# Windowed attention and a gated layer on one core: q and k of a head set in one transfer each, heads h and h+2 paired, far rows of v in one transfer, a few steps in another order

## The chip, the cores and the metric

The kernel runs on one core of a Trainium2 chip. The metric is device time in microseconds (us). Three runs of the kernel before took 621.86, 622.98 and 624.29 us; their median is 622.98 us. A profile is one more execution, recorded instruction by instruction. PE is the matmul engine (PEld its weight load), DVE the vector engine, ACT the scalar engine, POOL the general one, SP the engine that issues most transfers; SPq and ACTq are the issuing queues of SP and ACT.

## The reference, cut to what matters

```python
# q, k, v: 4 batches, 8 heads, 768 positions, 64 values a head; n_global = 8, n_local = 96
scores = q @ k.T / sqrt(64) - slope[h] * dist           # dist: i - j, or n_local for a global key outside the window
keep   = (j < n_global) | ((i - j >= 0) & (i - j < n_local))
a      = softmax(where(keep, scores, -1e9))
x      = (a @ v), heads side by side: 3072 x 512
h      = x @ w_in                                       # 3072 x 2048
g      = h * tanh(log1p(exp(h)))
out    = g @ w_out                                      # 3072 x 512
```

Since a position sees only the last 96 keys and the first few, scores are computed against a window of keys and 32 "far" keys from the start of the sequence.

## The kernel before, in words

The 3072 positions are cut into 12 chunks `ci` of 256 (three per batch), each of two blocks of 128. The heads of a chunk are cut into two sets `g` of four heads, so there are 24 loads of q and k, numbered `G = 2 ci + g`. `load_qk(G)` (step `q`, L161 to L176) brings a set into two tiles: `qr`, 128 partitions by 2 heads by 256 positions, and `kr`, 128 partitions by 2 heads by 416 keys. Partitions 0 to 63 hold the 64 values of one head of a pair (`j = 0`), partitions 64 to 127 those of the other (`j = 1`); `a2` numbers the two pairs. A pair is heads `2 a2` and `2 a2 + 1` of the set. q comes from `qT` by one transfer (L172) whose source pattern has the outer count 128; k comes from `kd`, which holds each head's 416 keys in order and holds them twice, by two transfers, one for each `j` (L175), each with the outer count 64. For the first chunk of a batch only keys from 128 on are loaded. The very first `j = 1` half goes through ACT's queue, all else through SP's. Each of `qr` and `kr` has three buffers.

For the first three chunks (`CF32`, loads 0 to 5) the score matmuls (`scores`, step `s`, L407) read `qr` and `kr` as they are, in f32. For later chunks `high_q`, `low_q`, `high_k`, `low_k` (steps `a` to `d`) first split them into f16 halves on ACT, DVE and POOL (`ws<-qr`, `wc<-kr`). Then `largest` (step `t`, L421, DVE) adds the mask and finds the row maximum, `exps` (`y`, L430, ACT) exponentiates, the weights are turned, by PE for the first chunks (`P`, L460, copied out by `F`) and by a DMA transpose later (`X`, L450, into `AT`), and `weigh` (`W`, L482 and L486, PE) multiplies by v. `window_v` (step `x`) gathers the v rows of the window; for the second and third chunk it reads the 32 far rows twice by two transfers (L234). The masks are made once, one 128 by 128 tile (`L`, tile `mb0`) and one 128 by 256 tile (`M`, tile `mb`) a head: on ACT, or, where a step carries a prime, on DVE for heads 0 to 3 and on POOL for heads 4 to 7 (`masked`, L284 to L288). The gated layer follows chunk by chunk: `i` (L549, `ph`), its activation on ACT and DVE, and `o` (L605, `po`). The weights come in 32 pieces of 512 KB (step `w`, L322 and L324) and are converted by ACT, DVE and POOL; step `B` (L353) is DVE's first touch of a piece.

Nothing is scheduled by a planner: a string `PROGRAM` lists all steps, and each engine and each queue does its part of them strictly in that order. SP's queue therefore holds the q, k, v and weight loads, the transposes `X` and `V` and the stores, in one line.

Of the kernel before, what the change touches and what calls it, by code (L numbers as in the profile page):

```python
# [16 lines left out]
ALU = mybir.AluOpType  # L17
# [3 lines left out]
P = 128  # L21
NLMAX = 97
NGMAX = 32
NPREV = 96
# [18 lines left out]
def tile_kernel(ctx, tc, qd, kd, qT, kT, v, n, w_in, w_out, out):  # L43
# [33 lines left out]
    with ExitStack() as st:  # L77
        windowed(st, tc, locals())
# [36 lines left out]
def windowed(st, tc, loc):  # L115


    nc = tc.nc
    L = NS()
    L.__dict__.update(loc)  # L120
    B, H, D, S, NB, NCC, NFB = L.B, L.H, L.D, L.S, L.NB, L.NCC, L.NFB
    CH, KW, DM, DFF = L.CH, L.KW, L.DM, L.DFF
    W = 2 * P
    GH = H // 2
    NCHB = S // CH
    NC = B * NCHB
    NFP = NFB // 2
    OWN = NPREV + NGMAX
# [16 lines left out]
    def copy(out, in_, scale, other=False):  # L145

        if other:
            nc.vector.tensor_scalar(out, in_, scale, None, op0=ALU.mult)  # L148
        else:
            nc.scalar.activation(out, in_, AF.Copy, scale=scale)  # L150
# [12 lines left out]
    def load_qk(G):  # L163
        if G >= 2 * NC:
            return
        ci, g = divmod(G, 2)
        b, c = divmod(ci, NCHB)
        o = OWN if c == 0 else 0
        pairs = slice(g * GH // 2, (g + 1) * GH // 2)
        qr = raws.tile([P, GH // 2, CH], F32, name="qr", bufs=3)  # L170
        kr = raws.tile([P, GH // 2, KW], F32, name="kr", bufs=3)
        nc.sync.dma_start(qr, L.qT[b].rearrange("(a j) d s -> (j d) a s", j=2)[:, pairs, c * CH:(c + 1) * CH])  # L172
        for j in range(2):
            half = slice(j * D, (j + 1) * D)
            (nc.scalar if G == 0 and j else nc.sync).dma_start(kr[half, :, o:], L.kd[ci, half].rearrange("p (a j) w -> p a j w", j=2)[:, pairs, j, o:])  # L175
        raw[G] = (qr, kr)  # L176

    def first_key(G):
        return OWN if (G // 2) % NCHB == 0 else 0
# [31 lines left out]
    def halves_v(tile_):  # L211
        return tile_.rearrange("p t m -> p (t m)").bitcast(F16).rearrange("p (t x m) -> p t x m", t=2, x=2)
# [10 lines left out]
    def window_v(ci):  # L223
        b, c = divmod(ci, NCHB)
        vc = stk.tile([P, 2, DM], F32, name="vc")
        if ci < CF32:
            far = L.v[b, 0:NGMAX, :]
            if c == 0:
                nc.sync.dma_start(vc[0:NPREV, 1], L.v[b, P - NPREV:P, :])
                nc.sync.dma_start(vc[NPREV:P, 1], far)  # L230
            else:
                nc.sync.dma_start(vc[0:NPREV], L.v[b, c * CH - NPREV:(c + 1) * CH - NPREV, :].rearrange("(t p) m -> p t m", p=P)[0:NPREV])
                for t in range(2):
                    nc.sync.dma_start(vc[NPREV:P, t], far)  # L234
            vcmp[ci] = vc
            return
        vo = vown[ci]
        vc = halves_v(vc)
        for t in range(2):
            if c == 0 and t == 0:  # L240
                continue
            src = vo[NGMAX:P, 0] if t else vown[ci - 1][NGMAX:P, 1]
            nc.sync.dma_start(vc[0:NPREV, t], src)
            nc.sync.dma_start(vc[NPREV:P, t], vo[0:NGMAX, 0] if c == 0 else vcmp[ci - 1][NPREV:P, 1])
        vcmp[ci] = vc


    UNIT = L.ISC
# [33 lines left out]
    mb0 = cp.tile([P, H, P], BF16, name="mb0")  # L282

    def masked(out, in_, h, other):  # L284
        if other and h >= H // 2:
            nc.gpsimd.tensor_scalar(out, in_, -L.slopes[h] * UNIT, None, op0=ALU.mult)
        else:
            copy(out, in_, -L.slopes[h] * UNIT, other)  # L288

    def mask_own(h, other=False):  # L290
        masked(mb0[:, h, :], d0, h, other)

    def mask_far(h, other=False):
        masked(mb[:, h, :], rel, h, other)
# [90 lines left out]
    def shape(t):  # L385
        ci, g, blk, a2 = where(t)
        first = ci % NCHB == 0 and blk == 0
        return ci, g, blk, a2, first, 1 if first else 2
# [21 lines left out]
    def largest(t):  # L410
        ci, g, blk, a2, first, nk = shape(t)
        w = nk * P
        sc = pend[t]
        if (ci, blk) not in stat:
            stat[ci, blk] = [at.tile([P, H], F32, name=f"{n}{blk}") for n in ("rs", "nm")]
        nm = stat[ci, blk][1]
        A = at.tile([P, 2, W], F32, name="A", bufs=3)
        for j in range(2):
            h = g * GH + 2 * a2 + j
            m = mb0[:, h, :] if first else mb[:, h, :]  # L420
            nc.vector.tensor_tensor_reduce(out=A[:, j, 0:w], in0=sc[j][:, 0:w], in1=m, scale=-1.0 / (UNIT if ci < CF32 else UNIT * SQ), scalar=3.0e38, op0=ALU.add, op1=ALU.min, accum_out=nm[:, h:h + 1])  # L421
        pend[t] = A

    def exps(t):
        ci, g, blk, a2, first, nk = shape(t)
        rs, nm = stat[ci, blk]
        A = pend[t][:, :, 0:nk * P]
        for j in range(2):
            h = g * GH + 2 * a2 + j
            nc.scalar.activation(A[:, j], A[:, j], AF.Exp, bias=nm[:, h:h + 1], scale=-1.0, accum_out=rs[:, h:h + 1])  # L430

    def halved(t):
# [36 lines left out]
    def weigh(t):  # L469
        ci, g, blk, a2, first, nk = shape(t)  # L470
        AT = pend.pop(t)
        if (ci, blk) not in pavs:
            pavs[ci, blk] = ps.tile([P, DM], F32, name=f"pav{blk}", bufs=1)
        pav = pavs[ci, blk]
        vs = [vown[ci][:, blk]] if nk == 1 else [vcmp[ci][:, blk], vown[ci][:, blk]]
        for j in range(2):
            h = g * GH + 2 * a2 + j
            cols = slice(h * D, (h + 1) * D)
            n, last = 0, 3 * nk - 1
            if ci < CF32:  # L480
                for kk in range(nk):
                    nc.tensor.matmul(pav[:, cols], AT[:, j * nk + kk, :], vs[kk][:, cols], start=(kk == 0), stop=(kk == nk - 1))  # L482
                continue
            for kk in range(nk):
                for x, y in ((0, 0), (0, 1), (1, 0)):
                    nc.tensor.matmul(pav[:, cols], AT[:, (x * 2 + j) * nk + kk, :], vs[kk][:, y, cols], start=(n == 0), stop=(n == last))  # L486
                    n += 1
# [149 lines left out]
    v1 = cp.tile([1, NALL], F32, name="v1")  # L637
# [4 lines left out]
    def checks(i):  # L642
# [22 lines left out]
    E = mybir.EngineType  # L665
    acts = {
        "q": load_qk, "v": load_v, "w": load_w,
        "a": lambda p, other=False: high_q(p - 1, other), "b": lambda p: low_q(p - 1), "c": lambda p, other=False: high_k(p - 1, other),
        "d": lambda p, other=False: low_k(p - 1, other), "N": units, "h": high_v, "l": low_v, "x": window_v,
        "K": lambda i: masks_far() if i else masks_own(), "L": mask_own, "M": mask_far,  # L670
        "s": scores, "t": largest, "y": exps, "g": high_a, "p": low_a, "X": turn_a, "W": weigh,
        "I": identity, "P": turn_p, "F": turned, "O": turn_x32,
        "R": rows, "T": high_x, "U": low_x, "V": turn_x,
# [2 lines left out]
        "z": high_g, "Z": low_g, "o": moe_out, "Q": evacuate, "Y": store, "f": lambda i: flags(), "k": checks,  # L676
    }
    PROGRAM = """
        I0 K0 L2 K1 L4 L0 L3 v0 w2 q1 x0 s0 t1 y1 M3 P1 L1' t0 s2 B2 F1' f0 M0 M2 M1 L5 y0 A2 t3 t2 P0 W1 y3 P3 q2 w0 v1 w1 q3 x1 s4 F0' M6' M4' M7' L7' M5'
        L6 F3' y2 P2 W3 t5 t4 S2' F2' y4 y5 s6 P4 P5 W0 W2 F4 t6 t7 y6 P6 s8 F6' C2 t9 t8 B0 S0 F5 y7 W6 W5 P7 W4 R0 B1 y9 A0 F7 y8 s10 P9 O0 W7 P8 t11 S1'  # L680
        t10 A1 C0 R1 F9 y11 F8 y10 P11 s12 P10 O1 w3 w4 q4 w7 w6 q5 w5 v2 w12 x2 w8 v3 w13 w10 w14 w9 w15 t12 t13 T0 F11 D2 D0 y12 y13 E2 E0 T1' U0 F10' U1
        W8 s14 W9 P12 i0 P13 t14 A3' B3 y14 S3 S4 F12' t15 B4 C3 y15 j0 u0 n0 F13 W10 P14 s16 W11 W13 P15 W12 G0 D3' C1 t17 D1 y17 A7 F15 S7 r0 B7 t16 F14'
# [6 lines left out]
        j12 A25' B19 E17 H11 S22' G12 A19 z11 C24 Z11' o3 i4 i17 D24 B22 E24 C22 E20 S19 u12 j4 D22 u4 n4 c7 n12 G4 S25' C19 B25 a7' C25 d7' b7 o11 s24 i18  # L689
        D19 r12 J17 r4 E22' H4 N0 t24 D25' A26' H12 t25 z4' J18 y25 A21 z12 E25' l3 E19' Z12' S26' B21 B26 Z4' i13 s26 i5 o12 j13 y24 G13 u13 S21 j5 A28 o4  # L690
        i20 q9 w30 w27 S28' C21 C26 D26' E26' B23 B28 t26 A30 u5 n5 D21 C28 g25 r5 n13 B30 G5 J20' S30' g24 E21' y26 r13 A23 H5 S23' i19 i6 p25' z5 A27 C23
        J19' D23 E23' c8' C30 H13 j6 u6 D28 g26 z13 B27 p26' Z5 Z13' D30' G6 E28' E30 p24 d8 w29 X25 w31 v4 X24 q8 x3 X26 i14 o5 i21 j14 u14 n6 r6 n14 S27
        r14 G14 H6 t27 S31 a8 i7 C27 y27 J21 z6 j7 u7 D27 B29 b8 S29' E27 Z6' H14 z14 Z14 i15 s28 o13 o14 o6 n7 r7 j15 u15 a9 n15 A31' A29' B31 G7 H7 t28
        C29 C31 G15 D31' z7' Z7' r15 D29 j16 u16 j17 y28 u17 n17 n16 r16 g27 H15 g28' p28' G16 z15' t29 E29 E31 H16 Z15 z16' G17 p27' Z16' o7 s30 o15 j18
        u18 y29 Q0 r17 q10 X28 Y0 o16 t30 g29' b9 H17 z17' Z17' h4' a11' t31 p29 y30 n18 r18 j19 u19 c9 G18 H18 d9' G19 z18' Z18 n19 Q1 r19 H19 j21 j20 o17
# [38 lines left out]
        n94 r94 o92 H94 j95 u95 G95 n95 z94 r95 o93 Z94 H95 z95 o94 k1 Z95' o95 k2 Q11  # L734
    """
    load_qk(0)
    nc.scalar.preload_act_table_set("natural_log_exp_and_others")
    with tc.manual_schedule(engines={E.DVE, E.Activation, E.Pool, E.PE, E.SP}):
# [156 lines left out]
```

## Time and profile before

| | us |
|---|---|
| median of three runs | 622.98 |
| the profiled execution's own time | 621.52 |
| its span in the trace | 619.7 |
| PE busy in it | 603.1 |
| DVE, ACT, POOL busy | 463.2, 444.8, 163.3 |
| PE's first matmul | 6.06 after the span's start |

The profiled execution's time is 1.8 us more than its span and 1.5 us under the median. In a row of the timeline the columns are start, duration, engine, line, operation, tiles written <- tiles read, shapes, count, and in brackets the idle time before it with what ended it. A row on waits reads: engine, line, what it waited for, total us, times, longest. A row on transfers reads: tiles, queue, count, KB each, median us from issue to landing. A row on a stretch of time has each engine's busy time, PE's clock, the share of the sixteen DMA engines that was busy and the GB/s they moved.

### The profile page before, as it was taken

The page shows a single profiled execution, that of the slowest core. Times are in us where ns is not written, and L with a number is a line of the kernel's source. Part 1 is how long each engine was busy: PE and PEld are TensorE (multiplying, and loading weights), DVE is VectorE, ACT ScalarE, POOL GpSimd, SP SyncE. Part 2 cuts the span into 40 slices and gives each one's busy share as a digit, 9 for nine tenths or more (in the row PEclk, how much of TensorE's full clock was granted, in tenths as well). Part 3 has the DMA queues.
Part 4 walks back from the last instruction along what each step waited for, and adds up shares of the span by engine and source line. Part 5 has one row for each costly group of instructions (what it writes and reads, how often), then busy time and mean ns, then how long its engine had stood idle before and what let it go on. Part 6 is the DMA issues. An engine that isn't in the chain of part 4 may idle for free.

```text
span 619.7 us, 13567 instructions
## 1 busy us (share of the span) xinstructions
PE 603.1 (97%) x5066; PEld 417.0 (67%) x5066; DVE 463.2 (75%) x1198; ACT 444.8 (72%) x1106; POOL 163.3 (26%) x135
## 2 busy tenths in 40 slices
PE   4999999999999999999999999999999999999996
PEld 3888857686556767576776775776667766766672
DVE  5899999989998789687776777775885866462443
ACT  5999888779886767576876757766866865665652
POOL 3031434033222350224133204223124332301020
PEclk9999999999999999999999999999999999999998
DMA  8998465235365859226357554474374344320001
GB/s 222 285 264 280 142 201 150 71 110 133 69 142 132 161 103 217 53 63 144 69 90 196 100 129 103 102 176 62 68 160 83 65 71 105 87 35 1 34 2 38
DMA packets 123014, 73.02 MB, mean 118 GB/s; under 512 B 91712, under 2 KB 112192, under 8 KB 122944
## 3 DMA queue, kind: packets, MB, share of 16 engines
q1 hardware_dynamic: 122800, 71.97, 49.8%
q8 instruction: 41, 0.67, 0.5%
q10 hardware_dynamic: 144, 0.15, 0.1%
q14 instruction: 29, 0.24, 0.1%
HBM read 39.85 MB, written 6.29 MB: 74 GB/s over the span
## 4 chain that ended last, share of the span: by engine, by line
PE 77%; DVE 11%; ACT 4%; issue 4%; DMA 2%; SPq 0%; POOL 0%; DVEq 0%; ACTq 0%; POOLq 0%
PE ph L549 33%; PE po L605 30%; PE sc L407 5%; PE pav L486 3%; PE pav L482 2%; DVE gf L587 2%; DVE gf L583 2%; DMA wts<-w_in 1%; DMA AT<-hl 1%; DVE ws L357 1%; PE po L460 1%; DVE A L421 1%; ACT A L430 1%; PE pav L605 1%; DVE ws L353 1%
## 5 line engine op out<-in xcount | busy, mean ns | idle before, releaser
L549 PE MATMUL ph<-xT,wts 128*128 128x256 f16 x2304 | 263.6, 273 | 0.2 <-POOL wts L154 0.2
L549 PEld LDWEIGHTS <-wts 128*128 128x128 f16 x2304 | 222.8, 98 | 35.5 <-issue 1.9
L605 PE MATMUL po<-wts,gt 128*128 128x512 f16 x1056 | 238.7, 379 | 0.8 <-DVE gt L148 0.5
L605 PEld LDWEIGHTS <-gt 128*128 128x128 f16 x1152 | 110.1, 98 | 126.8 <-issue 2.9
L154 POOL TENSOR_TENSOR gt<-gf,gt 128x512 f16<-128x512 f32 x55 | 67.5, 1229 | 278.7 <-DVE gt L148 142.7
L567 ACT ACTIVATE e<-ph 128x512 f32<-128x512 f32 x90 | 53.1, 590 | 89.9 <-PE ph L549 89.7
L430 ACT ACTIVATE A<-A,nm 128x256 f32<-128x256 f32 (+1 forms) x192 | 91.6, 478 | 29.1 <-DVE nm L421 29.1
L587 DVE CUSTOM_DVE_ANT_0 gf<-gf,u 128x512 f32<-128x512 f32 x96 | 79.5, 829 | 42.9 <-ACT u L579 41.7
L583 DVE SCALAR_TENSOR_TENSOR gf<-e,ph 128x512 f32<-128x512 f32 x90 | 61.1, 682 | 52.4 <-ACT e L567 51.3
L421 DVE CUSTOM_DVE_ANT_0 A<-sc,mb 128x256 f32<-128x256 f32 (+1 forms) x192 | 68.3, 396 | 16.9 <-PE sc L407 13.8
L154 POOL TENSOR_TENSOR hl<-A,hl 128x512 f16<-128x512 f32 (+1 forms) x36 | 44.8, 1250 | 74.2 <-DVE hl L148 31.8
L571 ACT ACTIVATE u<-e 128x512 f32<-128x512 f32 x96 | 59.9, 625 | 1.7
L579 ACT ACTIVATE u<-u 128x512 f32<-128x512 f32 x96 | 59.4, 624 | 1.8
L575 ACT ACTIVATE u<-u 128x512 f32<-128x512 f32 x96 | 59.5, 623 | 1.7
L154 POOL TENSOR_TENSOR wts<-ws,wts 128x512 f16<-128x512 f32 x20 | 25.7, 1292 | 72.1 <-ACT wts L150 37.6
L150 ACT ACTIVATE gt<-gf 128x512 f16<-128x512 f32 x44 | 27.4, 623 | 22.0 <-DVE gmax L587 22.0
L430 ACT ACTIVATION_READ_ACCUMULATOR A<-A,nm 128x1 f32 x192 | 36.0, 188 | 0.0
L486 PEld LDWEIGHTS <-AT 128*128 128x128 f16 x792 | 28.7, 98 | 7.2 <-issue 1.9
L154 DVE TENSOR_TENSOR hl<-A,hl 128x512 f16<-128x512 f32 (+1 forms) x36 | 30.0, 834 | 2.0 <-ACT hl L150 1.7
L154 DVE TENSOR_TENSOR gt<-gf,gt 128x512 f16<-128x512 f32 x41 | 28.9, 706 | 3.3 <-ACT gt L150 2.9
L407 PE MATMUL sc<-wc,ws 64*128 64x256 f16 (+1 forms) x432 | 28.2, 262 | 0.7 <-DVE nm L421 0.7
L486 PE MATMUL pav<-vo,AT 128*128 128x64 f16 x432 | 27.5, 193 | 0.0
(124 smaller groups left out, 600.3 us busy)
## 6 DMA issues: line engine op xcount, KB each, us to landing
kr<-kd SPq DMA_DIRECT2D x32, 208.0 KB, 4.2
qr<-qT SPq DMA_DIRECT2D x24, 256.0 KB, 4.2
wts<-w_in SPq DMA_DIRECT2D x12, 512.0 KB, 8.3
wts<-w_out SPq DMA_DIRECT2D x12, 512.0 KB, 8.9
out<-ob SPq DMA_DIRECT2D x11, 512.0 KB, 3.8
vr<-v SPq DMA_DIRECT2D x9, 512.0 KB, 5.1
vc<-vo SPq DMA_DIRECT2D x15, 192.0 KB, 3.3
kr<-kd SPq DMA_DIRECT2D x15, 144.0 KB, 5.1
```

The lines of the kernel that those rows point to most:

```text
L154: (nc.vector if other else nc.gpsimd).tensor_tensor(out, in_, high, op=ALU.subtract)
L407: nc.tensor.matmul(sc[j][:, a2, 0:w], x[half, a2, rows_], y[half, a2, col0:col0 + w], start=(n == 0), stop=(n == len(terms) - 1))
L421: nc.vector.tensor_tensor_reduce(out=A[:, j, 0:w], in0=sc[j][:, 0:w], in1=m, scale=-1.0 / (UNIT if ci < CF32 else UNIT * SQ), scalar=3.0e3 ...
L430: nc.scalar.activation(A[:, j], A[:, j], AF.Exp, bias=nm[:, h:h + 1], scale=-1.0, accum_out=rs[:, h:h + 1])
L486: nc.tensor.matmul(pav[:, cols], AT[:, (x * 2 + j) * nk + kk, :], vs[kk][:, y, cols], start=(n == 0), stop=(n == last))
L549: nc.tensor.matmul(ph[:, j, :].rearrange("p (b t) -> p b t", b=2), wv4[:, 2 * fb, x, c * P:(c + 1) * P], xT[:, :, y * NCC + c, :], start=( ...
L571: nc.scalar.activation(u, mish[m]["e"], AF.Square, bias=0.5)
L575: nc.scalar.activation(mish[m]["r"], mish[m]["u"], AF.Ln, bias=0.25 / RS, scale=1.0 / RS)
L579: nc.scalar.activation(r, r, AF.Exp, scale=-1.0)
L583: nc.vector.scalar_tensor_tensor(gf, mish[m]["e"], 0.5, mish[m]["h"], op0=ALU.add, op1=ALU.mult)
L587: nc.vector.tensor_tensor_reduce(out=gf, in0=gf, in1=mish[m]["r"], scale=SG / (SV * SW * RS), scalar=0.0, op0=ALU.mult, op1=ALU.max, accum ...
L605: nc.tensor.matmul(pos[ci][t], gt[:, x, j, t * P:(t + 1) * P], wv4[:, 2 * fb + 1, y, :], start=(fb == 0 and n == 0), stop=(fb == NFB - 1 a ...
```

## The change

1. `load_qk` issues one transfer for q and one for k. Both read packed arrays (`qd`, `kd`) through a hand-written source pattern with the counts 2, 64 and one run of 512 or 832 values: the outer count is the two halves of the partitions, the next one the 64 values of a head, and the run the two neighbouring heads of a half, 2048 bytes of q and 3328 of k. The destination is 128 partitions by the run. The first chunk's unused 128 keys are now loaded too (3328 instead of twice 1152 bytes a partition). The very first k goes through ACT's queue whole.
2. So that a half's heads are neighbours, a pair is now heads h and h+2 of the set (`head`): `j` picks the upper or lower two, `a2` the one of them. All steps that index heads follow.
3. The far rows of v for two blocks come by one transfer that reads them twice.
4. A primed mask is made on DVE for every head; POOL makes none.
5. In `PROGRAM`, `M3 L1'` stand ahead of `t1` instead of behind it, and `C30` ahead of `c8'` instead of behind it.

```diff
-        b, c = divmod(ci, NCHB)
-        o = OWN if c == 0 else 0
-        pairs = slice(g * GH // 2, (g + 1) * GH // 2)
         qr = raws.tile([P, GH // 2, CH], F32, name="qr", bufs=3)
         kr = raws.tile([P, GH // 2, KW], F32, name="kr", bufs=3)
-        nc.sync.dma_start(qr, L.qT[b].rearrange("(a j) d s -> (j d) a s", j=2)[:, pairs, c * CH:(c + 1) * CH])
-        for j in range(2):
-            half = slice(j * D, (j + 1) * D)
-            (nc.scalar if G == 0 and j else nc.sync).dma_start(kr[half, :, o:], L.kd[ci, half].rearrange("p (a j) w -> p a j w", j=2)[:, pairs, j, o:])
+        for dst, src, w, queue in ((qr, L.qd, CH, nc.sync), (kr, L.kd, KW, nc.sync if G else nc.scalar)):
+            both = bass.AP(src.tensor, ci * P * H * w + g * GH * w, [[D * H * w + GH // 2 * w, 2], [H * w, D], [1, GH // 2 * w]])
+            queue.dma_start(dst.rearrange("p a w -> p (a w)"), both)
         raw[G] = (qr, kr)
+
+    def head(g, a2, j):
+        return g * GH + j * (GH // 2) + a2
...
-                for t in range(2):
-                    nc.sync.dma_start(vc[NPREV:P, t], far)
+                nc.sync.dma_start(vc[NPREV:P], far.unsqueeze(1).broadcast_to([NGMAX, 2, DM]))
...
     def masked(out, in_, h, other):
-        if other and h >= H // 2:
-            nc.gpsimd.tensor_scalar(out, in_, -L.slopes[h] * UNIT, None, op0=ALU.mult)
-        else:
-            copy(out, in_, -L.slopes[h] * UNIT, other)
+        copy(out, in_, -L.slopes[h] * UNIT, other)
...
-            h = g * GH + 2 * a2 + j
+            h = head(g, a2, j)
...
     PROGRAM = """
-        I0 K0 L2 K1 L4 L0 L3 v0 w2 q1 x0 s0 t1 y1 M3 P1 L1' t0 s2 B2 F1' f0 ...
+        I0 K0 L2 K1 L4 L0 L3 v0 w2 q1 x0 s0 M3 L1' t1 y1 P1 t0 s2 B2 F1' f0 ...
...
```

SP's queue at the start of the program, before (loads 0 to 2; `vo` and `vc` are v, `wts` a weight piece; the half of load 0 that ACT issues is not in it):

```order
L62 DMA n_i<-n 128x4
L172 DMA qr<-qT 128x2x256
L175 DMA kr<-kd 64x2x288
L209 DMA vo<-v 128x2x512
L322 DMA wts<-w_in 128x4x256
L172 DMA qr<-qT 128x2x256
L175 DMA kr<-kd 64x2x288 x2
L229 DMA vc<-v 96x512
L230 DMA vc<-v 32x512
L172 DMA qr<-qT 128x2x256
L175 DMA kr<-kd 64x2x416 x2
```

The same place now:

```order
L62 DMA n_i<-n 128x4
L171 DMA qr<-qd 128x1x512
L208 DMA vo<-v 128x2x512
L317 DMA wts<-w_in 128x4x256
L171 DMA qr<-qd 128x1x512
L171 DMA kr<-kd 128x1x832
L228 DMA vc<-v 96x512
L229 DMA vc<-v 32x512
L171 DMA qr<-qd 128x1x512
L171 DMA kr<-kd 128x1x832
```

One transfer a load is gone from the line; load 0's k has left it altogether, and the shapes shown are those of the destination.

DVE before, from the copies of the turned weights of tiles 0 and 3 (`AT<-po`) to the row maxima of tile 5 (`po_196` and `po_204` are buffers of `po`, `mb_98` is the tile `mb0`, `nm` the maxima):

```order
L148 TENSOR_SCALAR AT<-po_196 128x256
L148 TENSOR_SCALAR AT<-po_204 128x512
L421 ISA A,nm_152<-sc,mb_98 128x128
L421 ISA nm_152 128x1
L421 ISA A,nm_152<-sc,mb_98 128x128
```

The same place now:

```order
L148 TENSOR_SCALAR AT<-po_194 128x256
L148 TENSOR_SCALAR mb<-e 128x256 x3
L148 TENSOR_SCALAR mb_98<-u 128x128
L148 TENSOR_SCALAR mb<-e 128x256
L148 TENSOR_SCALAR AT<-po_202 128x512
L416 ISA A,nm_152<-sc,mb_98 128x128
```

Five masks that POOL made stand now on DVE, between two copies for which PE's next `weigh` waits.

More of the change, by code (lines that the diff above doesn't have):

```diff
@@ L428, in exps @@
         for j in range(2):
-            h = g * GH + 2 * a2 + j
+            h = head(g, a2, j)
             nc.scalar.activation(A[:, j], A[:, j], AF.Exp, bias=nm[:, h:h + 1], scale=-1.0, accum_out=rs[:, h:h + 1])
@@ L476, in weigh @@
         for j in range(2):
-            h = g * GH + 2 * a2 + j
+            h = head(g, a2, j)
             cols = slice(h * D, (h + 1) * D)
@@ L678, in windowed @@
     PROGRAM = """
-        I0 K0 L2 K1 L4 L0 L3 v0 w2 q1 x0 s0 t1 y1 M3 P1 L1' t0 s2 B2 F1' f0 M0 M2 M1 L5 y0 A2 t3 t2 P0 W1 y3 P3 q2 w0 v1 w1 q3 x1 s4 F0' M6' M4' M7' L7' M5'
+        I0 K0 L2 K1 L4 L0 L3 v0 w2 q1 x0 s0 M3 L1' t1 y1 P1 t0 s2 B2 F1' f0 M0 M2 M1 L5 y0 A2 t3 t2 P0 W1 y3 P3 q2 w0 v1 w1 q3 x1 s4 F0' M6' M4' M7' L7' M5'
         L6 F3' y2 P2 W3 t5 t4 S2' F2' y4 y5 s6 P4 P5 W0 W2 F4 t6 t7 y6 P6 s8 F6' C2 t9 t8 B0 S0 F5 y7 W6 W5 P7 W4 R0 B1 y9 A0 F7 y8 s10 P9 O0 W7 P8 t11 S1'
@@ L691, in windowed @@
         i20 q9 w30 w27 S28' C21 C26 D26' E26' B23 B28 t26 A30 u5 n5 D21 C28 g25 r5 n13 B30 G5 J20' S30' g24 E21' y26 r13 A23 H5 S23' i19 i6 p25' z5 A27 C23
-        J19' D23 E23' c8' C30 H13 j6 u6 D28 g26 z13 B27 p26' Z5 Z13' D30' G6 E28' E30 p24 d8 w29 X25 w31 v4 X24 q8 x3 X26 i14 o5 i21 j14 u14 n6 r6 n14 S27
+        J19' D23 E23' C30 c8' H13 j6 u6 D28 g26 z13 B27 p26' Z5 Z13' D30' G6 E28' E30 p24 d8 w29 X25 w31 v4 X24 q8 x3 X26 i14 o5 i21 j14 u14 n6 r6 n14 S27
         r14 G14 H6 t27 S31 a8 i7 C27 y27 J21 z6 j7 u7 D27 B29 b8 S29' E27 Z6' H14 z14 Z14 i15 s28 o13 o14 o6 n7 r7 j15 u15 a9 n15 A31' A29' B31 G7 H7 t28
```

## The prediction

> **What bounds the kernel now.** I read the page's first two parts first, then the waits, then the transfers.
>
> ```profile
> PE 603.1 (97%) x5066; PEld 417.0 (67%) x5066; DVE 463.2 (75%) x1198; ACT 444.8 (72%) x1106; POOL 163.3 (26%) x135
> PE   4999999999999999999999999999999999999996
> ```
>
> PE is busy in all but the first and the last slice: what feeds PE is hidden except at the start. The waits say the same, PE's own row first:
>
> ```profile
> PE sc L407 <- DMA kr<-kd: 6.1, 1, 6.1
> PEld L486 <- DMA AT<-hl: 1.3, 3, 0.6
> DVE ws L353 <- DMA wts<-w_in: 2.1, 1, 2.1
> ```
>
> PE waits for a load of k once, at the start; all later loads of q and k come in time, and the transposes `AT` cost its weight load 1.3 us in all. So loads cost nothing as long as they stay quick. How quick they are, and how many engines carry them:
>
> ```profile
> q1 hardware_dynamic: 122800, 71.97, 49.8%
> q10 hardware_dynamic: 144, 0.15, 0.1%
> ...
> kr<-kd SPq DMA_DIRECT2D x32, 208.0 KB, 4.2
> qr<-qT SPq DMA_DIRECT2D x24, 256.0 KB, 4.2
> wts<-w_in SPq DMA_DIRECT2D x12, 512.0 KB, 8.3
> ...
> AT<-hl SPq DMA_TRANSPOSE x72, 3.3
> ...
> kr<-kd ACTq DMA_DIRECT2D x1, 144.0 KB, 3.6
> ```
>
> Queue q10 carried one transfer only, ACT's half of the first k: 64 partitions of 2 pieces are 128 packets, and 16 more stand there, one for each DMA engine that had a share to report. A transfer of 144 to 256 KB that is dealt out so lands in about 4 us.
>
> ```profile
> 9.50:15.50 6.00, 4.95 (x32) 3.23 (x30) 4.30 (x19) 4.21 (x17) 2.29 (x3) 1.00 1.10 233
> 16.50:18.50 2.00, 2.00 (x18) 1.62 (x19) 1.24 (x4) 1.73 (x8) 0.00 (x0) 1.00 1.06 393
> 62.00:558.00 496.00, 493.29 (x4275) 336.77 (x4275) 389.48 (x953) 363.24 (x892) 141.81 (x109) 1.00 0.50 112
> ```
>
> The last two columns are the busy share of the sixteen DMA engines and GB/s. Fully busy they move 393 GB/s at best, 24.6 per engine, and 233 in a worse stretch, 14.6 per engine. From 62 to 558 us they are half busy.
>
> **The change: one load of q and k.** It is now 128 partitions x (2048 + 3328) bytes = 688,128 bytes in two transfers. All that counts is over how many engines they are dealt out. Over sixteen it is 43,008 bytes each, 1.75 us (2.9 at the worse rate). Over two it is 344,064 bytes each, 14.0 us (23.6). No row of the trace shows a transfer of the new kind, so these are the ends. In every transfer of before the source and the destination begin with the same count (128, 96, 64 or 32), which sixteen divides. In the new ones the source begins with 2, the two halves, and the destination with 128. If a transfer is cut along that first count, the only equal cut that fits both is into two: partitions 0 to 63 by one engine, 64 to 127 by another. A cut into sixteen would need the queue to look through to the second count of one side only. I take two engines, at 24.6 GB/s (two engines alone crowd each other less than sixteen did in the worse stretch): 14.0 us a load.
>
> The Trainium skill, page "DMA: Bandwidth & Descriptors", section "Why a DMA increments its semaphore by 16 and not by 1", says it as a rule: a transfer from SP or ACT runs on the largest number of engines, at most 16, that divides the outermost count (other than 1) of both patterns. By the row of q10 alone the load would be 1.75 us on sixteen engines, by the rule 14.0 us on two. The trace agrees as far as it goes (64 and 64, sixteen reports); no run so far has an outer count under 16.
>
> **The start.** The first six loads feed PE directly. The first and the sixth use:
>
> ```profile
> 6.06 1.22 PE L407 MATMUL sc<-kr,qr 64*128 64x128 f32 x8 [6.06 <-DMA kr<-kd]
> ...
> 45.48 1.14 PE L407 MATMUL sc<-kr,qr 64*128 64x256 f32 x8
> ...
> 1.20 0.42 SPq L172 DMA_DIRECT2D qr<-qT  x1
> ```
>
> What a transfer takes beside its data: the q load issued at 285.8, in a quiet stretch, lands 3.0 us after its issue, and 256 KB at 393 GB/s are 0.7 us of that, so 2.3.
>
> ```profile
> DMA to landing us min/median/max: 3.0/3.0/3.0
> ```
>
> The first scores then start at 1.2 + 2.3 + 14.0 = 17.5, not 6.06. The loads stand in one line with v and weights. Up to the sixth load there are nine other transfers of 512 KB (1.33 us of each engine) and 0.77 MB of v windows (2.0 us): 14 us. It lands at 1.2 + 2.3 + 6 x 14.0 + 14 = 101.5 and is used at 45.5 now. PE's order is fixed and nothing later can go first, so the start costs 56 us; the other engines have no slack of that size, since each is in the same order behind the same scores.
>
> **The later eighteen loads.** Sum over the stretch 62 to 558: each engine is busy for 0.50 x 496 = 248 us; the two engines lose 18 x 1.75 and gain 18 x 14.0, and come to 468 of 496 us. So a load mostly fits, but never lands in under 2.3 + 14.0 = 16.3 us. Seven of the eighteen are used sooner after their issue, the first and the last of them:
>
> ```profile
> 139.59 0.57 SPq L172 DMA_DIRECT2D qr<-qT  x1
> ...
> 147.20 0.62 ACT L150 ACTIVATE ws<-qr 128x512 f16<-128x512 f32 x1
> ...
> 405.15 0.47 SPq L172 DMA_DIRECT2D qr<-qT  x1
> 412.34 0.61 ACT L150 ACTIVATE ws<-qr 128x512 f16<-128x512 f32 x1
> ```
>
> The seven gaps, from the issue to the first instruction on the tile, are 7.6, 10.6, 8.6, 12.9, 9.0, 6.8 and 7.2 us, 62.7 together, so 7 x 16.3 - 62.7 = 51 us are late even if each is alone in the line. They are not alone:
>
> ```profile
> 194.82 0.57 SPq L172 DMA_DIRECT2D qr<-qT  x1
> ...
> 201.43 0.58 SPq L172 DMA_DIRECT2D qr<-qT  x1
> ...
> 206.25 0.58 SPq L172 DMA_DIRECT2D qr<-qT  x1
> ...
> 208.26 4.43 SPq L450 DMA_TRANSPOSE AT<-hl  x2
> ...
> 216.93 0.25 PE L486 MATMUL pav<-vc,AT 128*128 128x64 f16 x3
> ...
> 402.36 0.72 SPq L172 DMA_DIRECT2D qr<-qT  x1
> ```
>
> Three loads issued within 12 us are 42 us of the two engines, to 194.8 + 2.3 + 42 = 239; the transposes issued at 208.3 stand behind them and are used by 216.9, 22 us too late, of which 5.7 is in the sum already. The load at 405.15 stands behind that at 402.36, 11 us more, and there is such a pair near 236 and a transpose behind a load near 432: some 49 us more together. Against that, ACT and DVE have a few us in hand when they stop, and each stop lets the line drain: 7 x 4 us less. Between 51 - 28 = 23 and 51 + 49 = 100 I take 85, near the upper end, since the two engines are 94% full there.
>
> **The small edits.** Masks: POOL's rows and the nearest DVE rows are
>
> ```profile
> 7.72 2.67 POOL L286 TENSOR_SCALAR mb<-e 128x256 bf16<-128x256 f32 x3 [6.24 <-DVE e L279]
> ...
> 7.88 0.32 DVE L148 TENSOR_SCALAR mb<-u 128x128 bf16<-128x128 f32 x1
> ...
> 13.66 0.42 DVE L148 TENSOR_SCALAR AT<-po 128x256 f32<-128x256 f32 x1
> 14.37 0.69 DVE L148 TENSOR_SCALAR AT<-po 128x512 f32<-128x512 f32 x1 [0.29 <-PE po L460]
> ```
>
> Four masks at 0.32 to 0.42 and one at 0.32 are 1.6 to 2.0 us on DVE, ahead of the copy at 14.37, where DVE had 0.29 free. The long wait for load 1 (to about 35 us instead of 14) covers them: 0. Without that cover they cost 1.3 to 1.7. `M3` and `L1'` ahead of `t1`: 0.3 on ACT and on DVE before the first maxima, covered by the 11 us wait for the scores, else 0.3. The swap of `C30` and `c8'` moves two neighbours on DVE: at most their 0.7 us either way, taken as 0. The far rows save two issues of about 0.3 us on SP, and the loads one issue each; nobody waits for SP's issuing today, so 0. The 128 KB more of each first chunk are in the 14.0.
>
> **Sum.** 621.5 (the profiled execution: span 619.7 and 1.8 around it) + 56 + 85 = 762.5, and 1.5 more for the median: 764 us.
>
> **The rivals.**
> - *Two engines, but only the start pays.* Loads are often issued far ahead, the DMA engines are half idle, and stops at one place give slack to the next. Then 623 + 56 = 679. Against it are the seven short gaps, which no idle time helps. 0.13.
> - *Two engines at the worse rate.* At 14.6 GB/s a load takes 23.6 us: the sixth lands at 159, 114 late, and the later stretch asks for 248 - 31 + 425 = 642 of 496 us, 146 late: 623 + 260 = 883. For it: rows of 9.5 to 15.5 us are of just such loads. Against it: fourteen engines are then out of the way. Anything over 825 has 0.10.
> - *The other side: sixteen engines after all.* If the queue cuts along the 128 partitions (or sees through the 2), a load takes 1.75 us and lands as now. Then SP issues the first weight piece 0.8 us sooner, behind 128 KB more (0.3 us), and DVE's wait for it, 2.1 us above, ends 0.5 sooner; the masks cost 1.3 to 1.7 behind it, partly under PE's own backlog. 623 - 0.5 + 0 to 1.7: about 623, no change. It decides at the very first k: q10 would show 128 + 16 packets instead of 128 + 2. For it: every row so far shows sixteen. Against it: every row so far also has equal first counts, and no cut into sixteen fits a first count of 2. 0.09.
>
> **How the numbers follow.** The forecast, 685 to 825, has 0.68. Its low end is a start of 45 (some transfers let through beside the loads) and 23 later with the median's 623, 691; its high end 60 and 140. With the rival at 679 the range 675 to 825 holds 0.81. About 0.5% (3.1 us) is what a measurement of this kernel can tell. Faster by more: 0.02, only within the last rival, if fewer and larger pieces free more than the masks cost. Same: 0.06, the rest of that rival but 0.01. Slower: 0.92.
>
> **What would show it.** Right: q10 with 130 packets; PE's first scores near 17.5 and the sixth load's near 101; loads that land 16 us or more after their issue; waits of PE on `sc` for DMA of some 50 us, then of ACT and DVE for `qr` and `kr` and of PE for `AT`. Wrong: 144 packets on q10 and loads that land in about 4 us (then the third rival), scores as late as said but no waits for loads after 110 us (the first), or a first load that takes 24 us (the second).

## The result and the profile after

The changed kernel takes 813.98 us, the median of six runs (810.60 to 816.46); the kernel before takes 622.42 us (six runs, 620.76 to 625.49). The ratio is 1.306, 95% interval 1.302 to 1.311. The forecast was 764, range 675 to 825. The profiled execution has a span of 814.7 us.

The page after, PE's busy time, its slices, the granted clock and the queue that carried the very first k:

```profile
PE 646.8 (79%) x5066; PEld 441.2 (54%) x5066; DVE 461.1 (57%) x1203; ACT 446.5 (55%) x1106; POOL 158.0 (19%) x130
PE   0575679996987980892996949899575899999997
PEclk9998579998997995795998989989878899999999
q10 hardware_dynamic: 130, 0.43, 0.2%
```

PE's row of nines has holes from the start to about 650 us (32 of the 40 slices). q10, which carries one transfer only, shows 128 pieces and 2 reports where it would show 16 for sixteen engines. The clock falls in the slices behind the holes; PE's busy time is 647 us instead of 603 for the same 5066 matmuls.

PE's waits after:

```profile
PE pav L481 <- DMA AT<-hl: 58.0, 7, 17.2
PE sc L402 <- DMA kr<-kd: 35.5, 5, 9.1
PE sc L402 <- DMA qr<-qd: 19.2, 1, 19.2
PE po L600 <- DVE gt L148: 11.8, 2, 11.0
PE pav L481 <- DMA vc<-vc: 11.7, 1, 11.7
```

The single wait of 6.1 us became 55 us for q and k at the start (`sc`), and 58 us for `AT`, the transposed weights, later. `AT` is no load of q or k: it is a transfer of another kind that comes late. The later loads of q and k are late too, for ACT and DVE, as all engines' waits after show:

```profile
DVE wc L148 <- DMA kr<-kd: 20.0, 1, 20.0
...
ACT ws L150 <- DMA qr<-qd: 15.6, 3, 13.7
```

The first scores and those that read the sixth load, in PE's timeline after:

```profile
19.21 1.23 PE L402 MATMUL sc<-kr,qr 64*128 64x128 f32 x8 [19.21 <-DMA qr<-qd]
...
109.73 2.08 PE L402 MATMUL sc<-kr,qr 64*128 64x256 f32 x8 [5.37 <-DMA kr<-kd]
```

They stood at 6.06 and 45.48 before: 13.2 and 64.3 us later. The stretches of the windows view show why. Its last three columns are PE's clock, the busy share of the sixteen transfer engines, and GB/s:

```profile
12.00:18.00 6.00, 0.00 (x0) 0.00 (x0) 0.00 (x0) 0.00 (x0) 0.00 (x0) 1.00 0.13 51
...
86.00:90.00 4.00, 0.00 (x0) 0.00 (x0) 0.00 (x0) 0.00 (x0) 0.00 (x0) 0.50 0.13 52
```

A share of 0.13 is 2 of 16 engines, and 51 GB/s are 25.5 each. PE, DVE, ACT and POOL do nothing in these stretches; two transfer engines alone are at work. In the second stretch the granted clock is 0.50, after the idle time ahead of it. The trace has no entry for the clock before 61 us, so the 1.00 of the first row is no reading: the eight matmuls on 64x256 at 22.11 take 2.08 us, as those at 109.73 do at half the clock, and 1.14 before.

SP's issuing at the start, in the timeline after (start, duration):

```profile
1.22 0.72 SPq L171 DMA_DIRECT2D qr<-qd  x1
1.98 0.42 SPq L208 DMA_DIRECT2D vo<-v  x1
2.45 5.38 SPq L317 DMA_DIRECT2D wts<-w_in  x1
7.87 6.55 SPq L171 DMA_DIRECT2D qr<-qd  x1
14.46 3.81 SPq L171 DMA_DIRECT2D kr<-kd  x1
```

Here an issue takes 0.4 to 0.7 us as long as the two engines have little in hand, then up to 6.6 us: SP is held up in the issuing itself. Its issues take 471.6 us together (231 of them), before 211.1 us (257).

To see where the 195 us arise, the start of some of PE's steps (`s`, `W`, `o` as in `PROGRAM`) in the trace after less that in the trace before: `s20`, on the sixth load, 64; `W24`, the first `weigh` on transposed weights, 85; `W39` 112; `W45` 132; `W57` 155; `W74` 194; the last step, 195. So 64 us come from the first six loads and some 130 us from the eighteen later ones, the last of which is issued at 614.

### The profile page after: what moved, and what is told of

The parts are those of the page before. It is cut to its first block, busy times and chain, and to the rows that moved or that the text cites. A ratio compares the mean times of both kernels' runs of the same rounds, so it can differ in the third digit from the quotient of the medians.

```text
span 814.7 us, 13523 instructions
## 1 busy us (share of the span) xinstructions
PE 646.8 (79%) x5066; PEld 441.2 (54%) x5066; DVE 461.1 (57%) x1203; ACT 446.5 (55%) x1106; POOL 158.0 (19%) x130
## 4 chain that ended last, share of the span: by engine, by line
PE 53%; DMA 30%; DVE 6%; SPq 5%; ACT 3%; issue 2%; POOL 0%; ACTq 0%; DVEq 0%; POOLq 0%
PE ph L544 23%; PE po L600 21%; DMA AT<-hl 11%; DMA kr<-kd 9%; PE sc L402 3%; DMA out<-ob 3%; DMA wr<-w_in 3%; PE pav L481 3%; DMA qr<-qd 2%; SPq L445 2%; DMA vc<-vc 2%; SPq L171 2%; PE pav L477 1%; DVE gf L582 1%; DVE gf L578 1%
## 5 line engine op out<-in xcount | busy, mean ns | idle before, releaser
L544 PE MATMUL ph<-xT,wts 128*128 128x256 f16 x2304 | 272.7, 278 | 9.6 <-DVE gf L578 9.4
L600 PE MATMUL po<-wts,gt 128*128 128x512 f16 x1056 | 250.6, 393 | 18.4 <-DVE gt L148 11.8
L544 PEld LDWEIGHTS <-wts 128*128 128x128 f16 x2304 | 227.3, 100 | 50.1 <-issue 12.6
L600 PEld LDWEIGHTS <-gt 128*128 128x128 f16 x1152 | 112.9, 100 | 153.7 <-issue 23.7
L481 PE MATMUL pav<-vc,AT 128*128 128x64 f16 x360 | 25.5, 197 | 66.9 <-DMA AT<-hl 55.2
L481 PEld LDWEIGHTS <-AT 128*128 128x128 f16 x792 | 30.5, 101 | 86.2 <-DMA AT<-hl 60.2
L402 PE MATMUL sc<-kr,qr 64*128 64x256 f32 (+1 forms) x96 | 21.4, 589 | 54.7 <-DMA kr<-kd 35.5
L154 POOL TENSOR_TENSOR wts<-ws,wts 128x512 f16<-128x512 f32 x20 | 26.1, 1315 | 139.3 <-ACT wts L150 85.5
L402 PEld LDWEIGHTS sc<-kr,qr 64*128 64x128 f32 x96 | 13.1, 298 | 58.3 <-issue 56.4
L481 PE MATMUL pav<-vo,AT 128*128 128x64 f16 x432 | 29.7, 199 | 11.0 <-ACT ob L613 8.1
L148 DVE TENSOR_SCALAR hl<-A 128x512 f16<-128x512 f32 (+1 forms) x41 | 18.7, 456 | 34.4 <-DMA AT<-hl 27.0
```

The source lines that it names most:

```text
L154: (nc.vector if other else nc.gpsimd).tensor_tensor(out, in_, high, op=ALU.subtract)
L402: nc.tensor.matmul(sc[j][:, a2, 0:w], x[half, a2, rows_], y[half, a2, col0:col0 + w], start=(n == 0), stop=(n == len(terms) - 1))
L544: nc.tensor.matmul(ph[:, j, :].rearrange("p (b t) -> p b t", b=2), wv4[:, 2 * fb, x, c * P:(c + 1) * P], xT[:, :, y * NCC + c, :], start=( ...
L600: nc.tensor.matmul(pos[ci][t], gt[:, x, j, t * P:(t + 1) * P], wv4[:, 2 * fb + 1, y, :], start=(fb == 0 and n == 0), stop=(fb == NFB - 1 a ...
```

## The experiments

`e2` to `e5`, `e8` to `e10` and `e12` were each executed once; their times stand beside 623.8 us (`e1`, ten executions), which has all of the change but the two engines.

**Sixteen engines by padding (e1), eight (e2), four (e3).** q and k are copied on the host into packed arrays whose 128 rows lie in 16, 8 or 4 groups, with a row of padding behind each, so that the source's first count is that number. All else is the change.

```diff
-            both = bass.AP(src.tensor, ..., [[D * H * w + GH // 2 * w, 2], [H * w, D], [1, GH // 2 * w]])
-            queue.dma_start(dst.rearrange("p a w -> p (a w)"), both)
+            part = (L.qp if src is L.qd else L.kp)[ci, g, :, 0:P // 16, :]     # counts 16, 8, one run
+            queue.dma_start(dst.rearrange("p a w -> p (a w)"), part)
```

> All of the change stays (one transfer each, 2048 and 3328 byte pieces, pairs h and h+2, masks, order); only the source's outermost count is 16 instead of 2, by packed arrays with a row of padding behind every eight rows. If a transfer is dealt out along that count: q10 shows 144 packets, a load lands in 4 to 6 us, and the time is 620 to 626 us. If it is the larger pieces, the nested pattern, the single transfer or the other order that are slow: it stays near 814.

> As the run with 16, with the outermost count 8. Dealt out along that count: q10 shows 136 packets, a load takes 3.5 us of eight engines, the first scores start near 7.0 us (1.2 + 2.3 + 3.5), the sixth load lands at 38.5, before its use at 45.5, and the time is 621 to 632 us. If any count under 16 falls back to one slow way: near 814.

> As the run with 16, with the outermost count 4. Dealt out along that count: q10 shows 132 packets, a load takes 7.0 us of four engines, the first scores start near 10.5 us, the sixth load lands at 59.5, 14 us late, and of the later loads five are late by 7 us together if each is alone: 645 us, up to 665 with queueing. If it falls back to one slow way: near 814.

Measured: 623.80 us with sixteen, ratio to before 1.001 (0.998 to 1.003); 642.33 with eight; 681.82 with four; 814.0 with the change's two. q10 in the four pages has 144, 136, 132 and 130 packets, 128 pieces and one report for each engine. With sixteen, transfers and waits look as they did before; a transfer's last column is us from issue to landing:

```profile
q10 hardware_dynamic: 144, 0.43, 0.3%
...
kr<-kp SPq DMA_DIRECT2D x23, 416.0 KB, 5.7
qr<-qp SPq DMA_DIRECT2D x24, 256.0 KB, 4.8
```

So the first count decides, and the rest of the change (pairing, masks on DVE, far rows, order) is worth nothing that can be measured. Both middle runs cost more than expected. The first scores wait until 10.7 us with eight engines and 14.4 with four, since the loads don't have these engines for themselves. Against the kernel before, PE is 13.4 us late at `s20` and 21.2 at the end with eight engines, 25.2 and 60.4 with four. With eight, in the windows view:

```profile
4.00:10.00 6.00, 0.00 (x0) 0.00 (x0) 3.09 (x13) 1.32 (x5) 0.00 (x0) 1.00 0.91 184
```

All sixteen are 91% busy, with v and weights too, at 184 GB/s, 12.6 per busy engine; the expectation had reckoned with the rate of a free one.

**Only the start on two engines (e4).** The change for loads 0 to 5, the packed arrays for the others.

```diff
+            if G < 6:
                 (the change's transfer)
+            else:
+                (the packed one)
```

> The first six loads as in the changed kernel, the later eighteen with the outermost count 16. If the start and the later loads cost separately: 622 + 64 = 686 us, since PE's use of the sixth load came 64 us later in the changed kernel. If the later stretch takes up the delay: under 660. If what follows the start is late for another reason than its own loads: over 720.

Measured: 687.44. Against the kernel before, PE's steps are 62.6 us late at `s20`, 65 from `W24` on, and stay so to the end (65.4).

**Only the later loads on two engines (e5).** The same with `if G >= 6`.

> The change, with the first six loads packed over sixteen engines and the later eighteen left on two. Theory: the start's loss and the later loads' loss add up. The whole change is 814.0, its start alone 687.4, so this is 814.0 - (687.4 - 623.8) = 750, 740 to 760; PE's steps are on time up to the sixth load (shift under 3 us) and lose about 130 us behind it. Rival: the later loads cost the 85 us of the forecast, and the rest comes from the two together (a line that is already long after the start): 700 to 715.

Measured: 747.15, that is 123.4 above `e1`; PE's steps are on time at `s20` and 125.2 us late at the end. With the start's 63.6 this makes 810.8 of the 814.0: the two parts add up, and the 85 of the forecast was too low by itself. PE's largest wait in this run, and SP's issuing ahead of the longest of its waits but one:

```profile
PE pav L485 <- DMA AT<-hl: 55.2, 6, 17.1
```

```profile
226.61 3.07 SPq L172 DMA_DIRECT2D kr<-kd  x1
229.84 10.75 SPq L449 DMA_TRANSPOSE AT<-hl  x1
240.64 0.52 SPq L172 DMA_DIRECT2D qr<-qd  x1
241.21 2.75 SPq L172 DMA_DIRECT2D kr<-kd  x1
244.06 14.14 SPq L449 DMA_TRANSPOSE AT<-hl  x2
```

A transpose that follows a load keeps SP for 10.8 us, the two of the last row for 10.4 and 3.7; PE's step on the second of them starts at 260.4, after 14.5 us of waiting.

**Two transfers by half (e6).** Each transfer of the change is cut into partitions 0 to 63 and 64 to 127, from the change's own arrays.

```diff
-            both = bass.AP(src.tensor, ..., [[D * H * w + GH // 2 * w, 2], [H * w, D], [1, GH // 2 * w]])
-            queue.dma_start(dst.rearrange("p a w -> p (a w)"), both)
+            for j in range(2):
+                part = bass.AP(src.tensor, ... + j * (D * H * w + GH // 2 * w), [[H * w, D], [1, GH // 2 * w]])
+                queue.dma_start(dst[j * D:(j + 1) * D].rearrange("p a w -> p (a w)"), part)
```

> The change, with each of the two transfers of a load cut by hand into its two halves of 64 partitions; arrays, pieces, order, masks and pairing are the change's. Theory: each transfer now begins with the same count of 64 on both sides and is dealt out over sixteen engines; q10 shows 64 + 64 packets and 16 for each of its two transfers, a load of q and k lands in about 5 us, and the time is 621 to 627, as with the packed arrays. Twenty-four loads issue two transfers more each, which nobody waits for. Rival: the size of the pieces or the larger transfers are the cause, and not the count of the outermost step: 750 to 815.

Measured: 626.16, ratio to before 1.004 (1.001 to 1.007); q10 has 160 packets (128 pieces and 16 reports for each of two transfers), and the pieces land quickly:

```profile
q10 hardware_dynamic: 160, 0.43, 0.3%
...
kr<-kd SPq DMA_DIRECT2D x46, 208.0 KB, 4.4
qr<-qd SPq DMA_DIRECT2D x48, 128.0 KB, 3.8
```

Twice the transfers, and 188 us faster than the change: their number was never the cost.

**PE kept at work in its waits (e7).** 1158 small matmuls on the masks are put ahead of twelve waiting steps, into the PSUM that the step then overwrites.

```diff
+    def fill(step, out):
+        for i in range(FILL.get(step, 0)):
+            nc.tensor.matmul(out, mb[:, 0, 0:P], mb[:, 1, 0:out.shape[-1]], start=True, stop=True)
```

> The change, with 1158 more matmuls on the masks ahead of twelve of PE's waiting steps (s4, s8, s12, s16, s20, i19, W24, W37, W39, W45, W57, W74), sized to 0.7 of the idle time in front of each; they write what the step itself writes next, so the outputs are the same. In the change's profile PE's busy time is 647 us where it was 603, and the granted clock falls to about half for some us behind the idle stretches. Theory A: those 44 us lie on the path, since PE has to work off what piled up; with PE kept at work the clock stays near 1.0 (mean over 0.95 instead of 0.904), PE's busy time less the added matmuls falls to 605 to 620, and the time falls by 20 to 45 us, to 770 to 795. Theory B: the loads set the pace whatever PE does, and the slow clock only fills time in which PE would have waited: 805 to 820 at a clock near 1.0.

Measured: 821.05, ratio 1.317 (1.311 to 1.324); not faster than the change. PE's groups of added matmuls (busy us, mean ns of one):

```profile
L410 PE MATMUL pav<-mb 128*128 128x64 bf16 x872 | 30.0, 201 | 8.1 <-ACT ob L623 8.1
...
L410 PE MATMUL sc<-mb 128*128 128x256 bf16 (+1 forms) x238 | 23.5, 259 | 0.0
...
L410 PE MATMUL ph<-mb 128*128 128x256 bf16 x48 | 6.9, 317 | 6.0 <-DVE gf L588 6.0
```

They take 60.4 us, less than meant (34 ns each on `pav`, where 60 had been reckoned), so the mean clock rose only from 0.904 to 0.925. (Both means count the time ahead of the trace's first clock entry as 1.00, 61 us in the change and 26 here, so the true rise is probably larger.) PE's busy time without them is 694.3 - 60.4 = 633.9 instead of 646.8: 13 us of PE's work became quicker. And little came of it: `s20` starts at 108.2 (109.7 in the change), `W39` at 333.0 (329.3), `W45` at 386.8 (382.8), `W74` at 634.9 (633.5). Two of the twelve fills spoil the comparison somewhat: those ahead of `i19` and of `W24` write what others still read, so they start only when the wait is over (the 6.0 and 8.1 us in the rows) and put 5.6 and 4.5 us on the path. The last step starts 1.8 us later than in the change, so a gain of up to some 8 us (an estimate: 5.6 + 4.5 - 1.8) may hide in this run, but not one of 20 to 45. Theory A falls as far as the fill reached; the loads set the pace, and the slow clock mostly fills time in which PE would have waited.

**The later loads issued by POOL (e8).** `e5` with `nc.gpsimd.dma_start` for loads 6 to 23.

> As the run with the later eighteen loads on two engines, but those eighteen (thirty-six transfers) are issued by POOL instead of SP, with the same patterns. Theory A: the pattern's outermost count decides on whichever queue it stands: 730 to 770, and the loads still land 16 us or more after their issue; SP is no longer held up in its issuing, so up to 20 us less than by SP. Theory B: only SP's and ACT's queues deal out by that count, and POOL's spreads its pieces over sixteen: loads land in about 5 us and the time is 622 to 650, the upper end if POOL's own work, 158 us of the span, delays the issues.

Measured: 717.48, under theory A's 730 to 770, far from B. The transfers, in this run's view:

```profile
q0 software_dynamic: 19008, 12.52, 7.6%
...
kr<-kd POOLq DMA_DIRECT2D x18, 416.0 KB, 14.0
...
qr<-qd POOLq DMA_DIRECT2D x18, 256.0 KB, 11.9
```

They still land late. In the trace of the first load (q issued at 85.5, k at 86.4) POOL's queue has four packets under way at a time from 89 to 93 us and two after that; the last two reports of q come at 93.8, those of k at 99.0 and 99.2. The windows view agrees with four engines and then two (the last two columns are the share of sixteen and GB/s):

```profile
90.00:93.00 3.00, 3.00 (x18) 1.64 (x16) 2.90 (x4) 2.31 (x5) 1.92 (x2) 1.00 0.23 90
94.00:98.00 4.00, 4.00 (x37) 3.39 (x36) 4.00 (x9) 1.36 (x3) 0.00 (x0) 1.00 0.13 52
```

So each transfer is on two engines here too, but q and k at the same time on different ones. The load is there 13 us after its issue. 29.7 us of the 123.4 are gone.

**The loads issued earlier, by SP (e9) and by POOL (e10).** In `PROGRAM` the steps `q6` to `q23` of `e5` and of `e8` are moved forward by 36 steps on average, two of them not at all.

```diff
-   ... i12 w28 q7 w23 ...           (q7 the 410th step)
+   ... q7 ...                       (now the 351st; the same for the other seventeen, by 0 to 60)
```

> As the run with the later eighteen loads on two engines (747.2), but their places in the program's order are moved forward, by up to 60 of its 1,900 steps, as far as the three buffers of q and k allow: mean 37 steps, some 12 us; 60, 57, 28 and 60 for four loads that stand 11 to 25 steps ahead of their use. Nothing else moves. Theory A: what costs is that a load needs 16 us and is issued 7 to 13 us ahead of its use; with the room given, the time falls to 670 to 700. Theory B: what costs is SP's line, in which the transposes of the weights stand behind the loads and SP itself is held up while it issues; the loads then meet other transposes and the time stays at 725 to 755.

> As the run with the later loads issued by POOL (717.5), with the loads moved forward by the same steps. SP's line and the short room are both taken away. If these two are the later loads' loss: 635 to 665. If theory A alone (short room): the same as the run by SP with early loads, within 15 us. If what costs is neither, but the work of the two engines itself (or fewer than sixteen) in the way of all other transfers: 695 to 720.

Measured: 738.39 by SP (8.8 less than `e5`) and 709.72 by POOL (7.8 less than `e8`). Room for a load is worth 8 to 9 us, not 50 to 75. Yet the room did what it was meant to do. This is what the engines waited for the later loads themselves in `e5`:

```profile
DVE wc L148 <- DMA kr<-kd: 19.8, 1, 19.8
...
ACT ws L150 <- DMA qr<-qd: 15.1, 3, 13.5
```

and this is all that is left of it in `e9`:

```profile
DVE wc L148 <- DMA kr<-kd: 4.5, 1, 4.5
```

ACT and DVE wait 30 us less for the loads, and the kernel gains 8.8. In `e10`, where the room is larger and no load stands in SP's line, PE still waits

```profile
PE pav L485 <- DMA AT<-hl: 34.9, 5, 16.6
PE ph L548 <- DMA xT<-xhl: 19.3, 3, 10.3
```

both for transposes, and these still keep SP, as one pair of them in SP's timeline shows:

```profile
253.40 0.57 SPq L212 DMA_DIRECT2D vr<-v  x1
257.60 1.23 SPq L531 DMA_TRANSPOSE xT<-xhl  x1
258.93 8.50 SPq L449 DMA_TRANSPOSE AT<-hl  x2
```

**The plain pattern (e11).** The second half of the partitions is laid out on the host with its heads rolled by two, so that one step leads through all 128 rows.

```diff
-            qs.append(np.concatenate([qb[:, :, c:c + 2 * P]] * 2, axis=0))
+            qs.append(np.concatenate([np.roll(qb[:, :, c:c + 2 * P], -j, axis=1) for j in (0, 2)], axis=0))
...
-  [[D * H * w + GH // 2 * w, 2], [H * w, D], [1, GH // 2 * w]]
+  [[H * w, P], [1, GH // 2 * w]]
```

> The change, with the second 64 partitions of q's and k's arrays laid out on the host with the heads rolled by two, so that one step covers all 128 partitions and the source's pattern is 128 x one piece, as the destination's; no padding, no more transfers than the change, all else of the change kept. Theory: sixteen engines; q10 shows 144 packets, a load lands in about 5 us, 621 to 627. Rival: pieces of this size behind a plain pattern are dealt out otherwise than with the padded arrays: 640 or more.

Measured: 623.11, ratio to before 1.000 (0.997 to 1.004), q10 with 144 packets, k landing in 5.6 and q in 4.9 us. No experiment gave a kernel that beats the one before.

**Dead transfers on two engines (e12).** All loads on sixteen engines as in `e1`; behind each of the later eighteen the same bytes once more, with the change's pattern, to a place in device memory.

```diff
+            if G >= 6:
+                both = bass.AP(src.tensor, ..., [[D * H * w + GH // 2 * w, 2], [H * w, D], [1, GH // 2 * w]])
+                queue.dma_start(L.spare[2 * G + (src is L.kd), :, 0:GH // 2 * w], both)
```

> All loads of q and k are packed over sixteen engines, as in the run of 623.8 us. Behind each of the later eighteen the same 688,128 bytes are moved once more by two transfers with the change's pattern (the source begins with 2, 128 pieces of 2048 and of 3328 bytes), from device memory to device memory, to a place that nobody reads. So no engine waits for a transfer on two engines; only what stands behind them, or shares engines with them, can be late. Theory A: the later loads cost time mostly by being in the way of others (transposes, weights, v, and SP's own issuing): 715 to 750, near the 747.2 of the run whose later loads were on two engines, with PE's waits for AT of 40 us or more. Theory B: they cost time because q and k themselves are late: 624 to 650. In between, the share of each is read off: (time - 623.8) of 123.4 us is what being in the way costs.

Measured: 775.50, 151.7 above `e1`, more than the 123.4 of `e5` and than the 750 expected at most. PE's largest wait:

```profile
PE pav L484 <- DMA AT<-hl: 75.8, 6, 20.2
```

Nobody waits for the dead transfers, and they cost all that the two-engine loads cost. The run doesn't take the lateness of q and k away altogether: real loads now stand behind dead ones (ACT waits 10.8 us for one `qr`, DVE 14.7 for one `kr`). That, and the 12.4 MB more that are moved, may be the surplus; it isn't explained one by one.

## Why the prediction was right in its mechanism and short by 50 us

- **Two engines.** Right. The Trainium skill, page "DMA: Bandwidth & Descriptors", section "Why a DMA increments its semaphore by 16 and not by 1", has the largest number up to 16 that divides both outermost counts; 130, 132, 136 and 144 packets for the counts 2, 4, 8 and 16 agree. The same section has POOL's queue take the same number of engines, but from a turning pointer, where SP's takes the lowest. `e8` agrees that two transfers in a row get different engines there (q ready at 93.8, k at 99.2); which ones by number no run here shows.
- **14.0 us a load.** Right. The two engines move 51 GB/s, 25.5 each against 24.6 forecast, so the data of a load are 13.5 us; the rival with 14.6 GB/s falls. With what stands ahead of it a load takes longer: the chain of the changed kernel has 21.1 us from the issue of the second load's k at 14.46 to its landing.
- **The start, 56 us.** 63.6 by `e4`. The first scores come at 19.2 instead of 17.5, the sixth load is used at 109.7 instead of 101.5. The step that is short is the 14 us for the nine other transfers and v: 109.7 - 1.2 - 2.3 - 6 x 14.0 = 22 us are left for them. SP's slow issuing, which puts them off, was in no term. How the 8 us divide was not tried.
- **The later loads, 85 us.** 123.4 by `e5`, above the 100 that was reckoned as its upper bound (the high end of the range had 140). The step that failed is the first one, the seven short gaps (51 us, "late even if each is alone in the line"): four such waits came, 35.6 us in the changed kernel, and `e9` takes all but 4.5 us of them away and gains 8.8. Not every gap could be lengthened there, and what `e9` has left isn't taken apart, but `e12` loses more than `e5` with no engine waiting for a transfer on two engines. The second step, the transposes behind the loads (49 us), named the mechanism and had the wrong size: PE's waits for `AT` alone are 58.0 us. Its reckoning took the bytes ahead in the line. It left out that SP itself stands still, so that all that follows it is late too, the transposes first.
- **"nobody waits for SP's issuing today, so 0."** True of today: by `e1`, the issues saved bring nothing. It is the sentence that hid the cost, since SP's issues became 260 us longer.
- **The small edits, 0.** Right as far as it can be told: 1.001 (0.998 to 1.003) in `e1`, with the cover of the long first wait gone. The 1.3 to 1.7 us that had been possible without it lie inside this interval.
- **"only the start pays"** falls by `e5`, **"sixteen engines after all"** by q10's 130 packets. What the latter gave as its time, 623, holds as soon as the pattern is even: three changed lines (`e11`) measure 623.1.
- **PE's clock** was in no term, and 44 us more of PE's busy time invite the thought that it is the missing 50. `e7` speaks against it, for the 13 us that its fills took off, all but some 8 us at most; the other 31 were not tried.

What stays open: of the later 123 us, POOL's issuing takes 30 away and the earlier place 8, which leaves 86 (`e10`), in which PE waits 54 us for transposes and SP is held up by them. Whether a transpose waits there for the two busy engines' data or for room to be issued was not told apart.

## What to carry to other kernels

Before merging transfers, write down the outermost count of both sides. Against 128 partitions, counts of 2, 4, 8 and 16 in the source gave as many engines here, and 64 or 128 on both sides gave sixteen. A transfer on two engines cost this kernel less by its own lateness than by what it did to everything that shared the queue and those engines. Two transfers with 64 rows each (626.2 us), or one with 128 rows in an even step (623.1), are within 0.7% of the transfers before; one with 2 x 64 is not (814.0). A count of packets on a queue with one transfer tells the number of engines at a glance.

## What the runs showed of the hardware beyond that

- An issue on SP is no fixed price: before the change 0.4 to 0.7 us for most transfers and 1.2 for a transpose, up to 12 us (a transpose, the longest in the change's trace) with two engines behind; for transposes also when the loads are issued by POOL (15.9 us for one in `e10`; 2.6 at most in `e1`).
- The granted clock stays at 0.50 behind PE's idle times: from 88 to 102 us PE is busy 11.9 of 14.0 us at 0.50, and its busy time grows from 603 to 647 us in all. The Trainium skill, page "TensorE: Matmul & The Clock Gate", section "Part 1: The HAM clock gate", has half the clock after about 3.4 us without work. The trace agrees with the half; here the clock falls at 85.0 us, 2.1 us after PE's last matmul ended (82.9). That the part of it which `e7` took away, 13 us of PE's work, cost some 8 us at most is what that run adds.
